# Top-32 attention and a squared-ReLU feed-forward: the next step's pair maxima ahead of the third search round, the far copy between the two exps

## The chip, the cores and the metric

The kernel runs on one core of a Trainium2 chip. The metric is the device time of one execution in microseconds (us), the median of several runs. The core has five engines with instruction queues of their own, each worked off in order: PE (TensorE, matmuls), DVE (VectorE), ACT (ScalarE), POOL (GpSimd) and SP (SyncE, which here issues DMAs). They wait for each other by semaphores.

## What is computed

For 8 batches of 8 heads with 576 rows of 64 values, attention in which each row keeps the 32 largest of its 576 scores; its result, 4608 rows of 512, goes through a feed-forward layer with a squared ReLU.

```python
def _attn_ref(q, k, v):
    top_k = 32
    scale = 1.0 / np.sqrt(D)
    scores = scale * np.matmul(q, k.transpose(0, 1, 3, 2))
    kth = np.partition(scores, -top_k, axis=-1)[..., -top_k:-top_k + 1]
    mask = scores >= kth
    scores = np.where(mask, scores, -1000000000.0)
    scores = scores - np.max(scores, axis=-1, keepdims=True)
    attn = np.exp(scores)
    attn = attn / (np.sum(attn, axis=-1, keepdims=True) + 1e-09)
    return np.matmul(attn, v)

def _moe_ref(x, w_in, w_out):
    h = np.maximum(x @ w_in, 0.0)
    return h * h @ w_out
```

## The kernel before

The 36864 rows of scores are worked in U = 144 steps of 256 rows: two tiles of 128 rows by 576 columns, called x = 0 and 1. `pin` keeps the instructions of each engine in the order in which the program issues them, so the order of the calls in the loop over u is the order of every queue.

**Scores.** In step u the scores of step u + 1 are made (`scores`): PE multiplies the first 288 columns into the PSUM tile sc_a and the other 288 into sc_b, and ACT copies each into the SBUF tile `s` (L299), with its sign turned in most steps (`sign`: positive only for u below 7 and in the last two steps). Between the two halves PE does the products of an older step (`in_gap`). sc_a and sc_b exist once: the next matmul into sc_a waits for its last reader, which is L324 (L322 where the sign is positive), that into sc_b for L353.

**The search for the 32 largest.** A tournament on DVE and POOL writes into the tile `cats`, which has one slot for even and one for odd steps.

- `pairs_of(u+1)` (L324 or L322, DVE): the larger of each column of sc_a and its partner in `s`, 288 for each tile, into `most`. It needs the copy of sc_b into `s`.
- `copy_far(u+1)` (L359, ACT): half of `most` back into the PSUM bank of sc_b.
- `quads_of(u+1)` (L352 and L353, DVE): the larger and the smaller of the two halves of `most`, into `cats`; the first of a step's operations on DVE, and it waits for the far copy.
- `both` (L367) and `lesser` (L375, POOL): sum of the pair less its larger one, which is the smaller one, into `cats`.
- `topk(u, rounds)`: rounds 0, 1 and 2 each find the eight largest (L406) of a part of `cats` for each tile and strike them out there (L410, a match-replace); round 3 finds the last eight. The parts grow: 100, 120, 151 and 368 columns. Before round 2 the eight largest of the lesser ones (L404) are put into columns TOP+QUAR to REST of the slot, which belong to the part of round 2, columns TOP to REST-1.

**After the search.** POOL marks in step u + 1 what falls away (`drop`, L470), and a DMA from POOL's queue adds the mark to `s` (`add_mask`, L474). Some steps later ACT does the exp of the two tiles (`exps`, L482; up to step U - 25 with the sum of each row as a second output, read by an instruction of its own), and SP's queue transposes the result by DMA into `wT` (`turn`, L491). The exps are those of step u - 3, in the last ten of step u - 2. Three, two and in the end again two steps later `products` multiplies wT with the values (`weigh`, L526), DVE takes a reciprocal (`invert`, L542 or L546) and ACT scales (`place`, L565, L570).

**`keep_tops`** (L442, ACT) copies, with its sign turned, the eight largest of round 0 and the eight lesser tops out of `cats` into `m_neg`: in each step where the sign is positive, for both slots at once in every odd step elsewhere. Its reading covers columns 0 to 8 and TOP+QUAR to REST.

**Other work between.** `prepare` puts transposed queries and keys (L180 and others), `dense` two or three pieces of the feed-forward (relu L661 and square L669 on ACT, L654 and L722 on PE) into each step, `fetch` loads the next heads on SP, `run_tests` and the list `tests` are small operations of POOL (L422).

The order of one step in the middle, by engine. DVE: quads, round 0, round 1, L404, round 2, L324 of the next step, round 3; the reciprocal stands ahead of round 1. ACT: copy of sc_a, a transposed x_tok where there is one, copy of sc_b, `prepare`, `place`, exp 0, exp 1, `keep_tops`, far copy, then values and the relu and square pieces. POOL: two drops, `both`, the mask's DMA, a test, `lesser`.

Of the kernel before, what the change touches and what calls it, by code (L numbers as in the profile page):

```python
# [23 lines left out]
def kernel(  # L24
# [9 lines left out]
    nc = tc.nc  # L34
# [8 lines left out]
    HALF, QUAR = S // 2, S // 4  # L43
    EIGHTH = S // 8
    TOP = 8
    REST = TOP + QUAR + 8
    LESS = REST + EIGHTH
    BACK = LESS + QUAR
    WIDE = REST + 3 * QUAR

    def pin(ins):
        tc.keep_in_program_order(ins)
        return ins
# [220 lines left out]
    st = {}  # L274
# [36 lines left out]
    def sign(u):  # L311
        return 1.0 if u < EARLY - 2 or u >= U - 2 else -1.0

    def pairs_of(u):
        d = st[u]
        cat = d["cat"]
        most = d["most"] = scp.tile([128, 2, HALF], f32, name="most", bufs=2)
        one, two = d["ps"][0], d["s"][:, :, HALF:S]

        def tt(to, lo, hi, op):  # L320
            if sign(u) > 0:
                pin(nc.vector.tensor_tensor(to, one[:, :, lo:hi], two[:, :, lo:hi], op=op))  # L322
            else:
                pin(nc.vector.scalar_tensor_tensor(out=to, in0=two[:, :, lo:hi], scalar=-1.0, in1=one[:, :, lo:hi], op0=ALU.mult, op1=op))  # L324

        if u:
            tt(most, 0, HALF, ALU.max)
        else:
            tt(d["ps"][1][:, :, 0:QUAR], QUAR, HALF, ALU.max)
            tt(most[:, :, 0:QUAR], 0, QUAR, ALU.max)  # L330
        if u < EARLY:
            tt(cat[:, :, BACK:BACK + QUAR], QUAR, HALF, ALU.min)
# [23 lines left out]
    def copy_far(u):  # L356
        d = st[u]
        if u:
            pin(nc.scalar.activation(in_two(d["ps"][1][:, :, 0:QUAR]), fours(u)[1], AF.Copy))  # L359
# [20 lines left out]

    def topk(u, rounds=(0, 1, 2, 3)):
        d = st[u]
        g = u % GROUP
        if g == 0 and 0 in rounds:
            held_m["last"] = (held_m.get("m"), held_m.get("neg"))
            held_m["m"] = small.tile([128, GROUP, 2, 3, 8], f32, name="m", bufs=2)
            held_m["neg"] = small.tile([128, GROUP, 2, 2, 8], f32, name="m_neg", bufs=2)
        held = held_m["m"]  # L390
        d["held_neg"] = held_m["neg"]
        m = d["m"] = [d["cat"][:, :, 0:TOP]] + [held[:, g, :, r] for r in range(3)]
        cat = d["cat"]
        def part(r, x):
            if r == 0:
                return cat[:, x, TOP:TOP + QUAR].rearrange("p (g n) -> p g n", n=36)[:, :, 0:25]
            if r == 1:
                return cat[:, x, TOP:TOP + QUAR].rearrange("p (g n) -> p g n", n=36)[:, :, 6:36]
            return cat[:, x, TOP:(REST - 1, BACK)[r - 2]]

        for r in rounds:
            if r == 2:
                for x in range(2):
                    pin(nc.vector.max(out=cat[:, x, TOP + QUAR:REST], in_=cat[:, x, BACK:WIDE]))  # L404
            for x in range(2):
                pin(nc.vector.max(out=m[r][:, x, :], in_=part(r, x)))  # L406
            if r == 3:
                break
            for x in range(2):
                pin(nc.vector.match_replace(out=part(r, x), in_to_replace=m[r][:, x, :], in_values=part(r, x), imm_value=NEG))  # L410
# [3 lines left out]
    def run_tests(u):  # L414
        f0 = 2 * (u + 1 - GROUP)
        both_held = held_m["last"] if u < U - 1 else (held_m["m"], held_m["neg"])
        held, neg = (both_held[z][:, :].rearrange("p g x r j -> p (g x) r j") for z in (0, 1))
        at = flags[:, :, f0:f0 + 2 * GROUP]
        least = held[:, :, 2, 7]

        def test(r, one, two, op):
            tests.append(lambda: pin(nc.gpsimd.tensor_tensor(at[:, r], one, two, op=op)))  # L422

        for r in range(2):
            test(r, least, held[:, :, r, 7], ALU.subtract)
        test(2, least, neg[:, :, 0, 7], ALU.add)
        test(3, held[:, :, 0, 0], neg[:, :, 0, 0], ALU.add)
        test(4, least, neg[:, :, 1, 7], ALU.add)
        test(5, least, least, ALU.mult)
# [46 lines left out]
    def exps(u, x):  # L476
        d = st[u]
        if u % 2 == 0 and x == 0 and u < SUMMED:
            d["sums"] = small.tile([128, 2, 2], f32, name="sums", bufs=4)
            st[u + 1]["sums"] = d["sums"]  # L480
        total = d["sums"][:, u % 2, x:x + 1] if u < SUMMED else None
        pin(nc.scalar.activation(w_two[u % 3][:, x, 0:S], d["s"][:, x, :], AF.Exp, bias=d["less"][x], scale=sign(u), accum_out=total))  # L482
# [55 lines left out]
    def invert(u):  # L538
        if u < SUMMED:
            if u % 2 == 0:  # L540
                both_r = small.tile([128, 2, 2, 1], f32, name="rboth", bufs=4)
                pin(nc.vector.reciprocal(both_r[:, :, :, 0], st[u]["sums"][:, :, :]))  # L542
                st[u]["r"], st[u + 1]["r"] = both_r[:, 0], both_r[:, 1]
            return
        r = small.tile([128, 2, 1], f32, name="rsum", bufs=4)
        pin(nc.vector.reciprocal(r[:, :, :], sums(u)[:, :, 64:65]))  # L546
        st[u]["r"] = r
# [324 lines left out]
    def ok(w):  # L872
        return 0 <= w < U
# [11 lines left out]
    def turn_x(u):  # L885
        for b, c in full:
            x_unit(u, b, c)
        full.clear()

    for u in range(U):  # L890
        at_step[0] = u
        for x in range(2):
            if ok(u - 1) and not by_vector(u - 1, x):
                drop(u - 1, x)
        quads_of(u)
        topk(u, (0,))
        if u == U - 1:
            break
        if ok(u + 1):
            for i, c, a in steps[u + 1]:  # L900
                while coming <= i or (coming == i + 1 and soon):
                    prepare(u)
            scores(u + 1, (lambda: in_gap(u)) if u else None)
            both(u + 1)
            if ok(u - 1) and by_dma(u - 1):
                add_mask(u - 1)
        if u == 0:
            in_gap(u)
        sums_late = ok(to_weigh(u)) and to_weigh(u) >= SUMMED and u < U - 5
        if sums_late:  # L910
            topk(u, (1,))
        if ok(to_weigh(u)):
            invert(to_weigh(u))
        casts_next = bool(soon) and soon[0].__name__ == "values"
        for _ in range(0 if casts_next else 2 if u < 8 else 1):
            prepare(u)
        if ok(to_weigh(u)):
            place(to_weigh(u))
        turn_x(u)
        moves.extend(soon_moves)  # L920
        soon_moves.clear()
        if u < 6:
            fetch(4)
        w = to_raise(u)
        if ok(w):
            exps(w, 0)
            exps(w, 1)
            turn(w)
        if u >= 6:
            fetch(4 if u < 12 else 3)  # L930
        if u and u % GROUP == 0:
            run_tests(u - 1)
        if tests and u % GROUP % 2:
            tests.pop(0)()
        topk(u, (2,) if sums_late else (1, 2))
        if u == U - 2:
            while behind:
                behind.pop(0)()
            take("d")
            products(u - 3)  # L940
            take("d")
        if ok(u + 1):
            pairs_of(u + 1)
            if u == U - 2:
                invert(u - 3)
            if sign(u) > 0:
                keep_tops(u, 1)
            elif u % 2:
                keep_tops(u, 2 if sign(u - 1) < 0 else 1)
            copy_far(u + 1)  # L950
            lesser(u + 1)
        if u == U - 2:
            place(u - 3)
            turn_x(u)
            take("d", True)
            moves.pop(0)()()
        if u == CATCH:
            exps(u - 2, 0)
            exps(u - 2, 1)
            turn(u - 2)  # L960
        topk(u, (3,))
        if casts_next:
            prepare(u)
        while after_far:
            after_far.pop(0)()
        after_far.extend(next_far)
        next_far.clear()
        if u < U - 2:
            dense(u, 0)
        if sign(u) > 0:  # L970
            st[u]["neg"] = negate(u, 3)
        if u in (SOON, CATCH + 1):
            w = to_weigh(u) + 1
            products(w)
            invert(w)
            place(w)
            turn_x(u)
        if u < U - 2:
            dense(u, 1)
        else:  # L980
            early_exps(u, 1)
        load_weights(1 if u else 2)
# [15 lines left out]
    exps(U - 2, 0)  # L998
    early_exps(U - 1, 0)
    early_exps(U - 1, 1)  # L1000
    topk(U - 1, (1, 2, 3))
    one.bits(8)
    mask(U - 2, 1)
    mask(U - 1, 0)
# [194 lines left out]
```

## Time and profile before

| | |
|---|---|
| median of 3 runs | 860.99 us (860.27 to 893.82) |
| the profiled execution's own time | 865.61 us |
| its span, first to last instruction | 863.8 us |
| mean granted TensorE clock in it | 0.959 |
| busy: DVE, ACT, POOL, PE | 819.9, 780.4, 770.6, 662.4 us |
| steps | 144 |

The profile is of one execution. Busy time is that of the instructions themselves; an engine's idle time is put down to what released it, which is inferred from semaphores. A line number is that of the listing above; where two shapes share a line, the shape tells them apart. In a timeline each row is one instruction, or several alike that follow each other (x2); the number in brackets at its end is the idle time just before it. DVE's instructions overlap a little with the one before, so start to start is shorter than the duration.

### The profile page before, as it was taken

To read this page: it belongs to the slowest core of one execution; us is meant where nothing else is said; L and a number is where in the kernel's file an instruction comes from. 1 tells how busy PE (TensorE), PEld (TensorE's weight loads), DVE (VectorE), ACT (ScalarE), POOL (GpSimd) and SP (SyncE) were. 2 spreads that over 40 slices of the span, in tenths; PEclk is the share of its full clock that TensorE was granted. 3 is DMA by queue.
4 is the path that set the end of the run, shared out by engine and by line. 5 is a ranking of instruction groups with operands and counts; after the bars stand their busy time and mean duration, and the time that the engine had idled before them with its cause. 6 is when DMAs were issued, how large, how long until landed. Compare 5 with 4: busy or idle time off the path is not lost.

```text
span 863.8 us, 20769 instructions
## 1 busy us (share of the span) xinstructions
PE 662.4 (77%) x6213; PEld 419.8 (49%) x6282; DVE 819.9 (95%) x3717; ACT 780.4 (90%) x1945; POOL 770.6 (89%) x830
## 2 busy tenths in 40 slices
PE   6787777877777877777787777777777878888886
PEld 3334344554555545444454454554444555555554
DVE  5999999998899999999999999999999999999994
ACT  4677799997999999999999999999999999999893
POOL 7999989997899999999899999999989998888881
PEclk9989999997999999999999999999999999999999
DMA  9999998799988999999988999989999998688861
GB/s 178 156 144 198 181 202 201 175 184 166 251 209 187 215 212 210 213 188 204 226 206 205 205 209 214 206 195 212 218 190 215 217 211 211 162 159 181 171 155 43
DMA packets 291064, 165.96 MB, mean 192 GB/s; under 512 B 258176, under 2 KB 268672, under 8 KB 290944
## 3 DMA queue, kind: packets, MB, share of 16 engines
q1 hardware_dynamic: 267408, 80.29, 51.3%
q0 software_dynamic: 22192, 83.83, 41.1%
q8 instruction: 52, 0.85, 0.4%
q14 instruction: 68, 0.56, 0.2%
q10 hardware_dynamic: 1344, 0.43, 0.2%
HBM read 37.75 MB, written 9.44 MB: 55 GB/s over the span
## 4 chain that ended last, share of the span: by engine, by line
DVE 41%; ACT 19%; issue 7%; PE 4%; DMA 4%; POOL 1%; ACTq 0%; DVEq 0%; POOLq 0%
DVE m L406 13%; DVE cats L410 12%; DVE cats L404 5%; DVE cats L352 3%; DVE cats L353 3%; ACT s L299 3%; DVE cats L406 3%; ACT w_two_c L482 2%; DMA wT<-w_two_b 2%; ACT w_two_a L482 2%; ACT rl L661 2%; ACT x_tok L565 2%; ACT w_two_b L482 2%; DMA wT<-w_two_c 2%; ACT sc_b L359 1%
## 5 line engine op out<-in xcount | busy, mean ns | idle before, releaser
L406 DVE MAX8 m<-cats 128x8 f32<-128x120 f32 (+2 forms) x864 | 281.6, 369 | 0.0
L367 POOL TENSOR_TENSOR cats<-s 128x576 int32<-128x576 int32 (+1 forms) x144 | 197.4, 1371 | 44.4 <-ACT s L299 37.0
L375 POOL TENSOR_TENSOR cats<-cats,most 128x576 int32<-128x576 int32 (+1 forms) x144 | 235.0, 1632 | 1.1 <-DVE most L324 0.2
L654 PEld LDWEIGHTS <-w_in 128*128 128x128 bf16 x2304 | 146.2, 101 | 41.2 <-issue 17.6
L290 PE MATMUL sc_a<-qkT 64*128 64x288 f32 x512 | 98.4, 462 | 86.5 <-DVE most L324 82.4
L410 DVE MATCH_REPLACE8 cats<-m,cats 128x120 f32<-128x120 f32 (+1 forms) x576 | 159.8, 286 | 0.0
L290 PE MATMUL sc_b<-qkT 64*128 64x288 f32 x512 | 103.9, 480 | 60.4 <-DVE cats L353 55.6
L722 PE MATMUL dn_ps<-w_out,h 128*128 128x512 bf16 x478 | 134.4, 400 | 9.7 <-issue 4.9
L654 PE MATMUL gen<-xT,w_in 128*128 128x128 bf16 x1984 | 136.5, 225 | 6.9 <-ACT xT L609 3.6
L299 ACT ACTIVATE s<-sc_b 128x576 f32<-128x576 f32 x144 | 93.4, 648 | 30.0 <-PE sc_b L290 25.4
L324 DVE SCALAR_TENSOR_TENSOR most<-s,sc_a 128x576 f32<-128x576 f32 x135 | 100.9, 747 | 0.7 <-ACT s L299 0.6
L299 ACT ACTIVATE s<-sc_a 128x576 f32<-128x576 f32 x144 | 91.4, 634 | 9.0 <-PE sc_a L290 7.2
L404 DVE MAX8 cats<-cats 128x8 f32<-128x216 f32 x288 | 95.3, 374 | 1.6 <-POOL cats L375 1.6
L290 PEld LDWEIGHTS sc_a<-qkT 64*128 64x128 f32 x512 | 39.9, 189 | 116.6 <-DVE most L324 99.8
L669 ACT ACTIVATE h<-rl 128x512 bf16<-128x512 f32 x136 | 85.7, 630 | 4.3
L661 ACT ACTIVATE rl<-gen 128x512 f32<-128x512 f32 x140 | 83.0, 593 | 2.4 <-PE gen L654 2.0
L526 PEld LDWEIGHTS <-wT 128*128 128x128 bf16 (+1 forms) x1600 | 55.1, 100 | 59.0 <-issue 46.8
L352 DVE TENSOR_TENSOR cats<-sc_b,most 128x288 f32<-128x288 f32 x144 | 64.6, 448 | 17.4 <-ACT sc_b L359 16.0
L290 PEld LDWEIGHTS sc_b<-qkT 64*128 64x128 f32 x512 | 43.3, 195 | 75.4 <-PE av_ps L526 40.9
L722 PEld LDWEIGHTS <-h 128*128 128x128 bf16 x544 | 49.9, 102 | 60.1 <-issue 24.6
L482 ACT ACTIVATE w_two_b<-s,m_neg 128x576 bf16<-128x576 f32 x95 | 72.5, 783 | 4.2 <-DMA s<-gone_b 2.3
L470 POOL TENSOR_SCALAR gone_a<-s,m 128x576 uint8<-128x576 f32 x90 | 66.9, 743 | 8.5
(203 smaller groups left out, 1487.2 us busy)
## 6 DMA issues: line engine op xcount, KB each, us to landing
s<-gone_b POOLq DMA_DIRECT2D x45, 576.0 KB, 4.8
s<-gone_c POOLq DMA_DIRECT2D x45, 576.0 KB, 4.8
s<-gone_a POOLq DMA_DIRECT2D x45, 576.0 KB, 4.4
v_raw<-in_v_dram SPq DMA_DIRECT2D x64, 128.0 KB, 3.3
k_raw<-in_k_dram SPq DMA_DIRECT2D x63, 128.0 KB, 3.9
q_raw<-in_q_dram SPq DMA_DIRECT2D x63, 128.0 KB, 4.2
out_dram<-wide SPq DMA_DIRECT2D x31, 256.0 KB, 3.4
v_raw<-in_v_dram SPq DMA_DIRECT2D x64, 32.0 KB, 3.9
```

Source lines behind the costliest of these rows:

```text
L290: pin(nc.tensor.matmul(out=ps[j][:, x, 0:HALF], lhsT=lhsT, rhs=rhs, start=True, stop=True))
L299: pin(nc.scalar.activation(s[:, :, j * HALF:(j + 1) * HALF], ps[j][:, :, 0:HALF], AF.Copy, scale=sign(u)))
L324: pin(nc.vector.scalar_tensor_tensor(out=to, in0=two[:, :, lo:hi], scalar=-1.0, in1=one[:, :, lo:hi], op0=ALU.mult, op1=op))
L367: pin(tt(less, s[:, :, 0:wide].bitcast(i32), s[:, :, HALF:HALF + wide].bitcast(i32), op=ALU.add))
L375: pin(tt(less, less, d["most"][:, :, 0:wide].bitcast(i32), op=ALU.subtract))
L404: pin(nc.vector.max(out=cat[:, x, TOP + QUAR:REST], in_=cat[:, x, BACK:WIDE]))
L406: pin(nc.vector.max(out=m[r][:, x, :], in_=part(r, x)))
L410: pin(nc.vector.match_replace(out=part(r, x), in_to_replace=m[r][:, x, :], in_values=part(r, x), imm_value=NEG))
L482: pin(nc.scalar.activation(w_two[u % 3][:, x, 0:S], d["s"][:, x, :], AF.Exp, bias=d["less"][x], scale=sign(u), accum_out=total))
L654: pin(nc.tensor.matmul(out=hp[:, n * n_rows:(n + 1) * n_rows], lhsT=w_in[:, kh, (f0 + n) * 128:(f0 + n + 1) * 128], rhs=xt(kh), start=(kh ...
L661: pin(nc.scalar.activation(kept["rl"][:, :], hp, AF.Relu))
L722: pin(nc.tensor.matmul(out=op[:, :], lhsT=held["h2"][:, f, c * 128:(c + 1) * 128], rhs=w_out[:, f, :], start=(f == 0), stop=(f == NF - 1)))
```

## The change

Three calls change places within a step of the loop; what each computes is as before.

- The eight lesser tops (L404) become a function of their own, `lesser_tops(u)`, which is called between rounds 1 and 2, where they were.
- `next_pairs(u)` holds what stood after round 2: `pairs_of(u+1)`, `keep_tops`, `copy_far(u+1)` and `lesser(u+1)`. It is now called right after `lesser_tops(u)`, ahead of round 2.
- The second exp and the transposing DMA (`exps(w, 1)`, `turn(w)`) and the loads of `fetch` come after `next_pairs(u)`. So on ACT `keep_tops` and the far copy stand between the two exps, and on DVE L324 stands ahead of round 2.
- In step U - 2 `next_pairs` keeps its old place, and the search of step U - 1 has its old order.

```diff
--- before.py
+++ after.py
@@ -380,6 +380,11 @@
 
 
 
+    def lesser_tops(u):
+        cat = st[u]["cat"]
+        for x in range(2):
+            pin(nc.vector.max(out=cat[:, x, TOP + QUAR:REST], in_=cat[:, x, BACK:WIDE]))
+
     def topk(u, rounds=(0, 1, 2, 3)):
         d = st[u]
         g = u % GROUP
@@ -399,9 +404,6 @@
             return cat[:, x, TOP:(REST - 1, BACK)[r - 2]]
 
         for r in rounds:
-            if r == 2:
-                for x in range(2):
-                    pin(nc.vector.max(out=cat[:, x, TOP + QUAR:REST], in_=cat[:, x, BACK:WIDE]))
             for x in range(2):
                 pin(nc.vector.max(out=m[r][:, x, :], in_=part(r, x)))
             if r == 3:
@@ -886,6 +888,17 @@
         for b, c in full:
             x_unit(u, b, c)
         full.clear()
+
+    def next_pairs(u, between=None):
+        pairs_of(u + 1)
+        if between:
+            between()
+        if sign(u) > 0:
+            keep_tops(u, 1)
+        elif u % 2:
+            keep_tops(u, 2 if sign(u - 1) < 0 else 1)
+        copy_far(u + 1)
+        lesser(u + 1)
 
     for u in range(U):
         at_step[0] = u
@@ -924,32 +937,28 @@
         w = to_raise(u)
         if ok(w):
             exps(w, 0)
+        if u and u % GROUP == 0:
+            run_tests(u - 1)
+        if tests and u % GROUP % 2:
+            tests.pop(0)()
+        if not sums_late:
+            topk(u, (1,))
+        lesser_tops(u)
+        if u < U - 2:
+            next_pairs(u)
+        if ok(w):
             exps(w, 1)
             turn(w)
         if u >= 6:
             fetch(4 if u < 12 else 3)
-        if u and u % GROUP == 0:
-            run_tests(u - 1)
-        if tests and u % GROUP % 2:
-            tests.pop(0)()
-        topk(u, (2,) if sums_late else (1, 2))
+        topk(u, (2,))
         if u == U - 2:
             while behind:
                 behind.pop(0)()
             take("d")
             products(u - 3)
             take("d")
-        if ok(u + 1):
-            pairs_of(u + 1)
-            if u == U - 2:
-                invert(u - 3)
-            if sign(u) > 0:
-                keep_tops(u, 1)
-            elif u % 2:
-                keep_tops(u, 2 if sign(u - 1) < 0 else 1)
-            copy_far(u + 1)
-            lesser(u + 1)
-        if u == U - 2:
+            next_pairs(u, lambda: invert(u - 3))
             place(u - 3)
             turn_x(u)
             take("d", True)
@@ -998,7 +1007,9 @@
     exps(U - 2, 0)
     early_exps(U - 1, 0)
     early_exps(U - 1, 1)
-    topk(U - 1, (1, 2, 3))
+    topk(U - 1, (1,))
+    lesser_tops(U - 1)
+    topk(U - 1, (2, 3))
     one.bits(8)
     mask(U - 2, 1)
     mask(U - 1, 0)
```

## Rows read from the trace of the kernel before

**Rows 1.** The page, busy us of each engine, share of the span, instructions.
```profile
PE 662.4 (77%) x6213; PEld 419.8 (49%) x6282; DVE 819.9 (95%) x3717; ACT 780.4 (90%) x1945; POOL 770.6 (89%) x830
```

**Rows 2.** Waits of DVE: engine, line, releaser, us in total, times, longest.
```profile
DVE cats L352 <- ACT sc_b L359: 16.0, 24, 2.1
```

**Rows 3.** Waits of ACT, the same columns.
```profile
ACT s L299 <- PE sc_a L290: 7.2, 13, 1.7
...
ACT m_neg L442 <- DVE cats L410: 1.5, 2, 1.0
```

**Rows 4.** Groups by line and form: count, busy us, mean ns, idle before.
```profile
L367 POOL TENSOR_TENSOR cats<-s 128x576 int32<-128x576 int32 x135 | 190.2, 1409 | 41.0 <-ACT s L299 33.7
```

**Rows 5.** Timeline of DVE around three steps: start us, duration us, instruction, idle before.
```profile
399.31 0.45 DVE L353 TENSOR_TENSOR cats<-sc_b,most 128x288 f32<-128x288 f32 x1
...
401.91 0.52 DVE L406 MAX8 m<-cats 128x8 f32<-128x151 f32 x2
402.35 0.07 DVE L410 MATCH_VALUE_LOAD cats<-m,cats 128x8 f32 x1
...
402.91 0.75 DVE L324 SCALAR_TENSOR_TENSOR most<-s,sc_a 128x576 f32<-128x576 f32 x1
403.57 0.98 DVE L406 MAX8 m<-cats 128x8 f32<-128x368 f32 x2
404.52 0.46 DVE L352 TENSOR_TENSOR cats<-sc_b,most 128x288 f32<-128x288 f32 x1
...
410.12 0.45 DVE L352 TENSOR_TENSOR cats<-sc_b,most 128x288 f32<-128x288 f32 x1
...
414.73 0.99 DVE L406 MAX8 m<-cats 128x8 f32<-128x368 f32 x2
415.63 0.45 DVE L352 TENSOR_TENSOR cats<-sc_b,most 128x288 f32<-128x288 f32 x1
```

**Rows 6.** Timeline of ACT in the first of those steps.
```profile
401.00 0.64 ACT L299 ACTIVATE s<-sc_b 128x576 f32<-128x576 f32 x1
401.53 0.60 ACT L180 ACTIVATE qkT<-gen 128x512 f32<-128x512 f32 x1
...
403.16 0.79 ACT L482 ACTIVATE w_two_b<-s,m_neg 128x576 bf16<-128x576 f32 x1
...
403.91 0.27 ACT L442 ACTIVATE m_neg<-cats 128x64 f32<-128x64 f32 x1
404.06 0.43 ACT L359 ACTIVATE sc_b<-most 128x288 f32<-128x288 f32 x1
```

**Rows 7.** Timelines of DVE and ACT in one of the last steps.
```profile
762.79 0.45 DVE L353 TENSOR_TENSOR cats<-sc_b,most 128x288 f32<-128x288 f32 x1
...
765.82 0.65 ACT L299 ACTIVATE s<-sc_b 128x576 f32<-128x576 f32 x1
...
766.51 0.75 DVE L324 SCALAR_TENSOR_TENSOR most<-s,sc_a 128x576 f32<-128x576 f32 x1
...
768.08 0.28 ACT L442 ACTIVATE m_neg<-cats 128x64 f32<-128x64 f32 x1
...
768.69 0.46 DVE L352 TENSOR_TENSOR cats<-sc_b,most 128x288 f32<-128x288 f32 x1 [0.53 <-ACT sc_b L359]
```

**Rows 8.** Timelines of DVE and POOL where L324 and L367 run together.
```profile
749.22 0.76 DVE L324 SCALAR_TENSOR_TENSOR most<-s,sc_a 128x576 f32<-128x576 f32 x1
...
749.26 1.41 POOL L367 TENSOR_TENSOR cats<-s 128x576 int32<-128x576 int32 x1 [1.30 <-ACT s L299]
```

**Rows 9.** Timelines of SP's queue and PE: a late transpose and its first user.
```profile
768.23 2.93 SPq L491 DMA_TRANSPOSE wT<-w_two_c  x1
...
776.85 0.48 PE L526 MATMUL av_ps<-vau_c,wT 128*128 128x65 bf16 x10 [1.05 <-DMA wT<-w_two_c]
```

**Rows 10.** Timeline of DVE: the first and last L352 of the 142 steps.
```profile
16.85 0.44 DVE L352 TENSOR_TENSOR cats<-sc_b,most 128x288 f32<-128x288 f32 x1
...
836.18 0.44 DVE L352 TENSOR_TENSOR cats<-sc_b,most 128x288 f32<-128x288 f32 x1
```

## The prediction

> **What bounds the kernel now.** I read the busy shares first. VectorE (DVE) works for 819.9 of 863.8 us, ScalarE (ACT) for 780.4, GpSimd (POOL) for 770.6 [rows 1]: three engines close together, DVE ahead. So a gain can only come out of DVE's idle time, and a loss comes as soon as DVE waits for an engine that has little to spare itself.
>
> DVE's list of waits comes next. One wait stands out: `quads_of` (L352) for the far copy of ACT (L359), 16.0 us in 24 waits [rows 2]. Third, the timeline of single steps. A step runs from one L352 to the next. An undisturbed one takes 5.51 us (410.12 to 415.63) [rows 5]; from the first L352 shown (16.85) to the last (836.18) 142 steps take 819.3 us, or 5.77 each [rows 10]. At 5.55 a step, with 0.36 more in the first seven for a second operation of `pairs_of`, 142 steps would need some 791 us. The rest, 29 us, is DVE waiting, some 27 of it for the two copies of ACT that are followed below. That is more than the 16.0 of the list, because a wait shorter than the running maximum's tail is swallowed by its busy time: in the step from 398.93 the two last maxima take 0.95 (403.57 to 404.52) where an undisturbed pair takes 0.90 (414.73 to 415.63) [rows 5].
>
> Fourth, ACT in the same step [rows 6]. It copies the scores of sc_b into `s` (L299, ending 401.64), then the copy of `prepare` (L180), then `place`, the first and the second exp (L482, the second at 403.16), `keep_tops` (L442, 403.91) and the far copy (L359, 404.06, ending 404.49). L352 starts at 404.52, 0.03 later: here the chain that sets the step is ACT's, from the copy of sc_b.
>
> **The change, part by part.** Nothing is added or removed; four groups change places.
>
> *The pair maxima (L324) go ahead of the third round.* DVE's sum stays: each DVE instruction starts where the one before lets it, and none of the new neighbours reads what its direct forerunner writes. L324 starts 1.00 earlier relative to the rounds (401.91 to 402.91 is the third round) [rows 5]. It needs the copy of sc_b, so that copy's deadline comes 1.00 earlier. In the shown step L324 could start at 401.91, and the copy ended at 401.64: no wait, 0.27 to spare. In the late step it ended at 766.47, 3.23 after the end of L353 (763.24), and L324 ran at 766.51 [rows 7]. L324's new place is 401.91 − 399.76 = 2.15 after L353's end, so a step like the late one waits up to 1.08 there that before it did not.
>
> *The lesser tops (L404) stay* between the second and the third round: L404's position to POOL's `lesser` is as before. Cost nothing. POOL's order (drops, `both`, the mask's DMA, a test, `lesser`) is also as before.
>
> *L324 beside POOL.* It now runs while POOL does `both` (L367). I take zero: with L324 at 749.22 and L367 at 749.26, L367 took 1.41 [rows 8], and its mean over 135 is 1409 ns [rows 4]. The bound on the other side would be L324's 0.66 on L367 in each of 134 steps, 88 us, and this row excludes it. The Trainium skill, "SBUF — State Buffer", section "SBUF: two separate sides", says that a DVE operation with two SBUF inputs and a GpSimd operation lock each other out for a whole instruction; read for any operation with two tensors, that would speak against this move. L324 takes one of its two from PSUM (sc_a), and by the rule as by the row it is free.
>
> *sc_a is freed 1.00 earlier.* ACT waited for PE's sc_a scores for 7.2 us in all [rows 3]; that is the most this can give, and nothing is the least. I take nothing, because most of ACT's copies of sc_a stand behind ACT's own relu and square.
>
> *Far copy ahead of the second exp.* The second exp's 0.75 (403.16 to 403.91) [rows 6] leaves the chain from sc_b's copy to L352 and comes behind the far copy. That is what can save the 16.0 us. It does not make ACT shorter: where ACT is behind, the exp is paid before the next step's copy of sc_b.
>
> *The transposing DMA (`turn`, SP's queue)* follows the second exp and comes later by the far copy, 0.43 at most [rows 6]. Behind it on SP stand the loads of `fetch` and the stores of `wide`; neither is needed within the step. Its product is: in the late steps the matmuls of `weigh` follow two steps after, and at 776.85 one waited 1.05 for a transpose issued at 768.23 [rows 9]. Bounds: nothing, or 0.43 in each of the last 21 steps (9 us). I take 0.4 us, for one such step.
>
> *A wait that the change makes.* `keep_tops` (L442) reads the lesser tops in columns TOP+QUAR to REST of `cats`; the third round's match-replace (L410) overwrites TOP to REST−1. They overlap. Before, `keep_tops` was issued after that L410 and waited for it: ACT's list has exactly this pair, L442 for L410 [rows 3]. After, it is issued ahead of it, so the order turns round: **DVE's L410 of the third round must wait until ACT's L442 has read.** This holds in each odd step, and in each of the first seven. Behind the waiting L410 stand the last maxima, L352, and through them POOL's drops and PE's next sc_b.
>
> Price in the shown step: L324 starts 401.91, the next instruction 0.66 later (402.91 to 403.57), L410's value load 0.44 after that (401.91 to 402.35): 403.01 [rows 5]. L442 starts at 403.91 − 0.75 = 403.16, ends 0.27 later at 403.43 [rows 6]; with 0.04 for the signal 403.47. **DVE waits 0.46.** From there 0.56 (402.35 to 402.91) and 0.90 to L352: 404.93 instead of 404.52. The far copy is long done (403.16 + 0.15 + 0.43), so its wait is gone and a longer one stands in its place: +0.41 for this step.
>
> In general this wait is (end of the sc_b copy + p + 0.04) − (start of L324 + 1.10), where p is ACT's way from that copy to L442's end without the second exp: 1.79 here, 1.22 in the late step (768.08 − 766.47 − 0.67 + 0.28, the late exps being 0.67 without their accumulator) [rows 6, 7]. With a prepared copy in the way (p about 1.8) it is 0.1 to 0.3 where sc_b comes early and 0.7 where it is just in time or late; without one it is nothing to 0.2.
>
> **The sum.** The same working, from step to step, each carrying ACT's place into the next, over the 142 steps from 16.85 to 836.18 [rows 10]:
> Waits before: 24.7 at L352 (16.0 of them in the list) and 2.1 at L324, together 26.8.
> After, at L410: 15.6 in the 35 odd middle steps with a prepared copy, 2.5 in the 22 without, 1.6 in the first seven, 2.1 in the last 21: 21.9.
> After, at L324: 5.0 in odd and 1.6 in even middle steps, 8.0 in the last 21, 0.2 early: 14.8. At L352 1.6 are left.
> 38.4 − 26.8 = **+11.6 us**. With 0.05 more or less for the signal the sum runs from +7 to +14.
>
> The profiled execution took 865.61 us (span 863.8), 4.6 above the median of 860.99. A stretch around 200 us in which PE ran slow holds 6 of its waits and 0.9 of the 11.6. Without it, and with the 0.4 for the transposes, the median goes from 861.0 to **872 us**, 1.3% slower.
>
> **Rivals.**
> *The wait is hidden* (0.20). If L442 ends within 1.10 of L324's start, the L410 term is nothing. For it: without a prepared copy it is nearly so. Against it: the shown step misses it by 0.42 before any signal [rows 5, 6]. What is left is 14.8 + 1.6 against 26.8, but without L410's wait DVE runs ahead of ACT and meets sc_b late in more steps and for longer: the same working without the L410 term gives −2 us, 859.
> *The far copy's waits simply go* (0.08). L352's 16.0 vanish and nothing takes their place: 845 us; with the hidden ones 836. For it: the largest wait on the list. Against it: the deadline of sc_b, 1.00 earlier, already missed in the late step [rows 7]. It decides if the copy of sc_b comes within 2.15 of L353 in nearly all steps.
> *The transposes come late too* (0.15). The 0.43 in each of the last 21 steps, and the next copies of sc_b late behind PE, add 9 to the 11: 881 us. For it the 1.05 of [rows 9], against it that few products waited at all.
> My forecast has 0.57.
>
> **How the numbers follow.** The range takes in the hidden wait below and the late transposes above, 857 to 881; what is left out is the case of 845 and the upper half of the last one. The forecast's own range is 867 to 876. Two per cent, about what a measurement of this kernel tells from no change, is 17 us: faster than 844 is the better half of the second rival, 0.03; slower than 878 is the third with a share of the forecast's tail, 0.17; in between 0.80.
>
> **What would show it.** DVE's list: L352 for L359 falls from 16.0 to under 3; a new line, L410 for ACT's L442, of about 22 us in some 60 waits, all in odd steps or the first seven; L324 for ACT's L299 appears with some 15, half of it in the last 21 steps. DVE's busy sum stays at 820, L367 at 1.41. The forecast is wrong if L410 shows no wait for L442, or if the odd and the even steps are equally long.

## The result: 872.4 us, 1.3% slower, odd steps longer and even ones shorter

The changed kernel takes 872.36 us (median of 6 runs, 870.40 to 876.23) where the kernel before, beside it, takes 861.73: a ratio of 1.013, 95% interval 1.011 to 1.015. In a later series it was 872.57 against 862.26, 1.013 (1.009 to 1.016). By two per cent that is no change; the intervals leave no doubt that it is slower. A run more than 1.5% above the fastest of the same kernel counts in the medians and not in the ratios. The granted TensorE clock is not what differs: the profiled execution of the later series had 0.960, that of before 0.959.

The profiled execution of the changed kernel took 873.15 us, its span is 871.3. Lines below 386 have kept their numbers. The lesser tops are now L386, the rounds' maxima L408, their match-replaces L412 (L410 before), `keep_tops` L444 (L442), the exps L484 (L482).

The page of the changed kernel, busy us, share of the span, instructions; [rows 1] is its like:

```profile
PE 667.2 (77%) x6213; PEld 424.8 (49%) x6282; DVE 822.2 (94%) x3717; ACT 781.5 (90%) x1945; POOL 770.5 (88%) x830
```

DVE, ACT and POOL do the same work within 2.3 us; the time that was added is waiting. DVE's list of waits for L324 in the kernel before (us in total, times, longest):

```profile
DVE most L324 <- ACT s L299: 0.6, 2, 0.3
```

and DVE's list in the changed kernel:

```profile
DVE cats L412 <- ACT m_neg L444: 11.5, 26, 0.7
DVE most L324 <- ACT s L299: 9.2, 18, 1.6
...
DVE most L322 <- ACT s L299: 1.6, 2, 1.2
```

The line of [rows 2], L352 for the far copy with its 16.0 us, is gone from the list. Two others stand in its place: the match-replace that waits for `keep_tops`, and L324, which waits for the copy of sc_b (0.6 us before).

The timeline of DVE in the step from 400.96, the same step of the computation as the first of [rows 5]:

```profile
400.96 0.43 DVE L352 TENSOR_TENSOR cats<-sc_b,most 128x288 f32<-128x288 f32 x1
...
403.93 0.73 DVE L324 SCALAR_TENSOR_TENSOR most<-s,sc_a 128x576 f32<-128x576 f32 x1
404.58 0.52 DVE L408 MAX8 m<-cats 128x8 f32<-128x151 f32 x2
405.51 0.09 DVE L412 MATCH_VALUE_LOAD cats<-m,cats 128x8 f32 x1 [0.41 <-ACT m_neg L444]
405.59 0.30 DVE L412 MATCH_REPLACE8 cats<-m,cats 128x151 f32<-128x151 f32 x1
...
406.10 0.98 DVE L408 MAX8 m<-cats 128x8 f32<-128x368 f32 x2
406.99 0.44 DVE L352 TENSOR_TENSOR cats<-sc_b,most 128x288 f32<-128x288 f32 x1
...
412.57 0.44 DVE L352 TENSOR_TENSOR cats<-sc_b,most 128x288 f32<-128x288 f32 x1
```

and of ACT in it, beside [rows 6]:

```profile
403.04 0.64 ACT L299 ACTIVATE s<-sc_b 128x576 f32<-128x576 f32 x1
403.57 0.60 ACT L180 ACTIVATE qkT<-gen 128x512 f32<-128x512 f32 x1
...
404.44 0.80 ACT L484 ACTIVATE w_two_b<-s,m_neg 128x576 bf16<-128x576 f32 x1
405.11 0.23 ACT L484 ACTIVATION_READ_ACCUMULATOR w_two_b<-s,m_neg 128x1 f32 x1
405.20 0.28 ACT L444 ACTIVATE m_neg<-cats 128x64 f32<-128x64 f32 x1
405.35 0.44 ACT L359 ACTIVATE sc_b<-most 128x288 f32<-128x288 f32 x1
```

L444 ends at 405.48; DVE's value load begins at 405.51, 0.03 later. The step is 6.03 us long (400.96 to 406.99), the even one after it 5.58 (406.99 to 412.57). The far copy ended at 405.79, 1.2 us ahead of the L352 that needs it: it comes early, as the change wanted, but it is no longer what DVE waits for.

Read from one L352 to the next, for all steps: the 57 odd steps of the middle (9 to 121) took 325.6 us before and 339.8 after, +14.2; the 57 even ones 325.2 and 318.1, −7.0; the last 21 126.8 and 126.2; the first seven 41.7 and 41.9. 1.2 us were lost before the first step of these. Five of the middle steps (31 to 35) lay in a slow stretch of the profiled execution of before, 33.8 against 30.3 us; there the granted TensorE clock was 0.70 of full speed from 200 to 210 us and 0.66 from 210 to 220. Without them the odd steps grew by 14.5 us and the even ones shrank by 3.8. The two profiled executions lie 7.5 us apart (865.61 and 873.15), without these five steps 11.1, near the distance of the medians (10.6).

### The profile page after: what moved, and what is told of

Read it like the earlier page. It is cut to its first block, busy times and chain, and to the rows that moved or that the text cites. A ratio compares the mean times of both kernels' runs of the same rounds, so it can differ in the third digit from the quotient of the medians.

```text
span 871.3 us, 20844 instructions
## 1 busy us (share of the span) xinstructions
PE 667.2 (77%) x6213; PEld 424.8 (49%) x6282; DVE 822.2 (94%) x3717; ACT 781.5 (90%) x1945; POOL 770.5 (88%) x830
## 4 chain that ended last, share of the span: by engine, by line
DVE 38%; ACT 31%; PE 15%; issue 10%; DMA 4%; POOL 1%; SPq 1%; ACTq 0%; DVEq 0%
DVE cats L412 11%; DVE m L408 10%; ACT s L299 6%; PE sc_b L290 6%; DVE cats L353 4%; DVE cats L352 4%; ACT x_tok L567 4%; ACT w_two_c L484 3%; DVE most L324 3%; ACT w_two_b L484 3%; ACT w_two_a L484 3%; DVE cats L386 3%; ACT rl L663 3%; PE gen L656 2%; PE sc_a L290 2%
## 5 line engine op out<-in xcount | busy, mean ns | idle before, releaser
L408 DVE MAX8 m<-cats 128x8 f32<-128x120 f32 (+2 forms) x864 | 281.8, 368 | 0.0
L367 POOL TENSOR_TENSOR cats<-s 128x576 int32<-128x576 int32 (+1 forms) x144 | 197.6, 1372 | 52.1 <-ACT s L299 47.5
L375 POOL TENSOR_TENSOR cats<-cats,most 128x576 int32<-128x576 int32 (+1 forms) x144 | 238.2, 1654 | 0.7
L656 PEld LDWEIGHTS <-w_in 128*128 128x128 bf16 x2304 | 150.9, 103 | 42.0 <-issue 20.5
L412 DVE MATCH_REPLACE8 cats<-m,cats 128x120 f32<-128x120 f32 (+1 forms) x576 | 159.1, 284 | 0.1
L724 PE MATMUL dn_ps<-w_out,h 128*128 128x512 bf16 x478 | 138.9, 410 | 10.1 <-issue 5.1
L656 PE MATMUL gen<-xT,w_in 128*128 128x128 bf16 x1984 | 139.6, 228 | 5.5 <-ACT xT L611 2.8
L299 ACT ACTIVATE s<-sc_b 128x576 f32<-128x576 f32 x144 | 93.5, 649 | 41.6 <-PE sc_b L290 32.2
L290 PE MATMUL sc_a<-qkT 64*128 64x288 f32 x512 | 100.5, 471 | 11.4 <-DVE most L324 10.2
L324 DVE SCALAR_TENSOR_TENSOR most<-s,sc_a 128x576 f32<-128x576 f32 x135 | 99.7, 739 | 9.3 <-ACT s L299 9.2
L386 DVE MAX8 cats<-cats 128x8 f32<-128x216 f32 x288 | 94.9, 371 | 1.6 <-POOL cats L375 1.6
L484 ACT ACTIVATE w_two_a<-s,m_neg 128x576 bf16<-128x576 f32 x96 | 75.2, 784 | 0.7 <-DMA s<-gone_a 0.7
L484 ACT ACTIVATE w_two_b<-s,m_neg 128x576 bf16<-128x576 f32 x95 | 74.0, 779 | 1.2 <-issue 1.2
L472 POOL TENSOR_SCALAR gone_c<-s,m 128x576 uint8<-128x576 f32 x90 | 66.9, 743 | 8.5
```

The costliest lines, as they stand in the source:

```text
L290: pin(nc.tensor.matmul(out=ps[j][:, x, 0:HALF], lhsT=lhsT, rhs=rhs, start=True, stop=True))
L299: pin(nc.scalar.activation(s[:, :, j * HALF:(j + 1) * HALF], ps[j][:, :, 0:HALF], AF.Copy, scale=sign(u)))
L367: pin(tt(less, s[:, :, 0:wide].bitcast(i32), s[:, :, HALF:HALF + wide].bitcast(i32), op=ALU.add))
L375: pin(tt(less, less, d["most"][:, :, 0:wide].bitcast(i32), op=ALU.subtract))
L472: pin(nc.gpsimd.tensor_scalar(byte[:, x, :], s[:, x, :], scalar1=d["m"][3][:, x, 7:8], scalar2=HUGE, op0=ALU.add, op1=ALU.mult))
L656: pin(nc.tensor.matmul(out=hp[:, n * n_rows:(n + 1) * n_rows], lhsT=w_in[:, kh, (f0 + n) * 128:(f0 + n + 1) * 128], rhs=xt(kh), start=(kh ...
```

## The experiments

Two rivals stand against the wait of the match-replace: that the earlier deadline of sc_b's copy costs the time (L324's 9.2 us), and that the second exp and the transpose behind it come too late. On the chip of the first four runs (the two with `keep_tops` elsewhere, the pair maxima with both exps ahead of `keep_tops`, and the far copy alone) most runs of the kernel before lay between 862 and 874 us, so their medians are read against 862.3 (before) and 872.6 (changed) of the second group, and the ratios measured beside them are given too.

### keep_tops behind the third round again

The lines that call `keep_tops` go from `next_pairs` into a function `keep(u)`, and this is called behind the third round:

```diff
     def next_pairs(u, between=None):
...
-        if sign(u) > 0:
-            keep_tops(u, 1)
-        elif u % 2:
-            keep_tops(u, 2 if sign(u - 1) < 0 else 1)
...
         topk(u, (2,))
+        keep(u)
```

> The changed order, but keep_tops (ACT) is issued behind the third round's match-replace again, as in the kernel before. Theory (the new wait of L410 for keep_tops costs the time): the changed kernel's waits of L410 for ACT's keep_tops (11.5 us in 26) are gone, L324's waits for the copy of sc_b grow a little (9.2 to about 13 us), and the time falls from 872 to about 858, 3 below the kernel before (range 855 to 862). Rival 1 (the earlier deadline of the sc_b copy costs it): L410's wait was only the same lateness seen later in the step, L324's wait takes it over, time stays at 868 to 873. Rival 2 (the second exp and the transpose come too late): nothing changes for them, 870 to 874.

Measured: 858.51 us (858.15 to 861.66; 0.989 of the kernel before, 0.983 to 0.995). Its DVE waits, the same columns:

```profile
DVE most L324 <- ACT s L299: 11.1, 22, 1.6
```

The wait for `keep_tops` is gone and 14 us with it. L324's wait grew by 1.9 us and did not take its place. Both rivals fall as the cause of the loss: sc_b's deadline is here as in the changed kernel, and so is the place of the second exp (0.15 us earlier, since `keep_tops` now stands behind it).

### keep_tops ahead of the first exp

`next_pairs` is without `keep_tops` here too.

```diff
+        if not sums_late:
+            topk(u, (1,))
+        lesser_tops(u)
+        if u < U - 2:
+            keep(u)
         w = to_raise(u)
         if ok(w):
             exps(w, 0)
...
-        if not sums_late:
-            topk(u, (1,))
-        lesser_tops(u)
```

> The changed order, but keep_tops stands ahead of the first exp on ACT, so that it reads the lesser tops 0.75 us sooner and the match-replace behind it need not wait. The far copy and the second exp stay where the change put them. Theory: L410's wait falls from 11.5 to 0 to 3 us, L324's wait is 10 to 14 us, time 859 (856 to 863). Rival 1 (sc_b's deadline): 868 to 873. Rival 2 (late transposes): 870 to 874.

Measured: 859.34 us (857.45 to 860.70; 0.988, 0.980 to 0.996). Its DVE waits:

```profile
DVE most L324 <- ACT s L299: 12.8, 24, 1.6
...
DVE cats L412 <- ACT m_neg L444: 0.3, 1, 0.3
```

Here the match-replace does stand behind `keep_tops`, as in the changed kernel, but that one comes 0.75 us sooner, and the wait falls from 11.5 us in 26 to 0.3 in one. It is the lateness of the read that costs, not the order as such.

### The pair maxima alone, both exps ahead of keep_tops

```diff
         if ok(w):
             exps(w, 0)
+            exps(w, 1)
+            turn(w)
...
         if u < U - 2:
             next_pairs(u)
-        if ok(w):
-            exps(w, 1)
-            turn(w)
```

> Only the first half of the change: L324 and next_pairs ahead of the third round, but both exps ahead of keep_tops and the far copy on ACT, as before. Theory: the match-replace of the third round now waits for a keep_tops that stands behind both exps, 0.75 us later in each odd step; L410's waits grow from 11.5 us to 40 to 65 us, in nearly all 71 odd steps, and the time is 895 to 918. Rival 1 (only sc_b's deadline): L324's waits as in the changed kernel, 864 to 873. Rival 2 (late transposes): the exps are back, so 860 to 863.

Measured: 922.15 us (920.06 and 924.25; 1.061, 1.050 to 1.072). DVE's waits, and then DVE's and ACT's timelines in one odd step:

```profile
DVE cats L412 <- ACT m_neg L444: 62.8, 71, 1.9
...
DVE most L324 <- ACT s L299: 4.9, 10, 1.0
DVE cats L352 <- ACT sc_b L359: 4.0, 9, 0.6
```

```profile
404.07 0.78 ACT L484 ACTIVATE w_two_a<-s,m_neg 128x576 bf16<-128x576 f32 x1
404.74 0.21 ACT L484 ACTIVATION_READ_ACCUMULATOR w_two_a<-s,m_neg 128x1 f32 x1
404.83 0.26 ACT L444 ACTIVATE m_neg<-cats 128x64 f32<-128x64 f32 x1
...
405.12 0.09 DVE L412 MATCH_VALUE_LOAD cats<-m,cats 128x8 f32 x1 [0.88 <-ACT m_neg L444]
```

With `keep_tops` one exp later the wait grows to 62.8 us, and the time by 50 us over the changed kernel (4 over the upper end of what was expected). It takes place 71 times, and the middle steps show where: 6.64 us an odd step, 5.67 an even one. The granted clock was lower here, 0.921, but DVE did not wait more for PE's scores: L324 waits 4.9 us for the copy of sc_b, where it is 9.2 in the changed kernel. That the rounds' order alone were the cause would have left this kernel at 864 to 873.

### The pair maxima alone, with nothing waiting for keep_tops

Again `next_pairs` is without `keep_tops`.

```diff
             exps(w, 0)
+            exps(w, 1)
+            turn(w)
...
         topk(u, (2,))
+        keep(u)
```

> L324 ahead of the third round as in the changed kernel, both exps ahead of the far copy as before the change, and keep_tops behind the third round, so that no match-replace waits for it. Against the run with the first half of the change alone only keep_tops is moved. Theory: the 62.8 us that L410 waited there are gone, L324 waits some 6 to 10 us, L352 still about 9 us for the far copy, time 861 (858 to 865), as the kernel before: what the pair maxima's move takes at L324 it gives back at L352. Rival (the earlier deadline of sc_b alone makes the kernel slower): 866 to 873.

Measured: 864.34 us, the median of ten runs from 859.39 to 879.39 (the profiled one took 861.65); 1.002 of the kernel before (0.998 to 1.006). DVE's waits:

```profile
DVE most L324 <- ACT s L299: 8.5, 17, 1.5
...
DVE cats L352 <- ACT sc_b L359: 3.6, 11, 0.6
```

Between the last two kernels only the place of `keep_tops` differs: 58 us. The move of the pair maxima by itself is worth nothing that these runs can tell: 8.5 us at L324 stand against what L352 no longer waits (16.0 before, 3.6 here, where about 9 was expected).

### The far copy alone

```diff
         lesser_tops(u)
+        topk(u, (2,))
         if u < U - 2:
             next_pairs(u)
         if ok(w):
             exps(w, 1)
             turn(w)
...
-        topk(u, (2,))
```

> Only the second half of the change: the far copy and keep_tops stand between the two exps on ACT, but L324 stands behind the third round as before. Theory: keep_tops reads after the third round again, so there is no wait of L410, and the copy of sc_b has its old deadline; L352's 16.0 us of waits fall to about 8, ACT waits a little for L324. Time 856 (853 to 860). Rival 1 (sc_b's deadline is what cost the time): the same, 853 to 860. Rival 2 (the late transposes cost it): as slow as the changed kernel, 868 to 874.

Measured: 856.31 us (854.12 to 857.65; 0.986, 0.980 to 0.992). DVE's waits, then ACT's longest:

```profile
DVE most L324 <- ACT s L299: 4.0, 7, 1.0
DVE cats L352 <- ACT sc_b L359: 3.5, 10, 0.6
```

```profile
ACT sc_b L359 <- DVE most L324: 17.5, 42, 0.9
```

This half of the change is a gain by itself: L352's wait falls from 16.0 to 3.5 us (8 was expected). ACT now often reaches the far copy before L324 is done and waits, 17.5 us in all; DVE's 3.5 at L352 is much less, so most of that waiting did not hold DVE up. The second exp and the transpose come late here too, in a kernel faster than the one before: it is shown twice that they are not what costs.

### The changed kernel again, and two places between

> The changed kernel as it is, for a comparison with the next three on one chip. Both theories expect what was measured: about 872 us (868 to 878), L410 waiting about 11 us for keep_tops in the list of waits.

Measured: 872.57 us, 1.013 (1.009 to 1.016). DVE's waits:

```profile
DVE cats L412 <- ACT m_neg L444: 12.0, 25, 1.1
DVE most L324 <- ACT s L299: 8.4, 18, 1.6
```

The next kernel calls `next_pairs`, without `keep_tops`, from within the third round, between its maxima and its match-replaces, and `keep` behind it; the second exp stays behind the far copy.

```diff
-        if u < U - 2:
-            next_pairs(u)
+        topk(u, (2,), (lambda: next_pairs(u)) if u < U - 2 else None)
         if ok(w):
             exps(w, 1)
             turn(w)
...
-        topk(u, (2,))
+        keep(u)
...
             for x in range(2):
+                if between and x == 0:
+                    between()
                 pin(nc.vector.match_replace(...))
```

> L324 between the maxima and the match-replaces of the third round (0.57 us instead of 1.00 earlier than before the change), the far copy between the exps, keep_tops behind the third round. Theory: no wait of L410; L324 waits for sc_b about 9 us instead of 11, L352 about 3; time 855 (852 to 858), the fastest or level with the version that moves the far copy alone (856.3). Rival (any earlier L324 costs, so the far copy alone is best): 857 to 860.

Measured: 854.72 us (854.31 to 857.47), 0.992 (0.989 to 0.995). With `x == 1` instead, between the two match-replaces:

> As the run before this one, with L324 between the two match-replaces of the third round (0.29 us earlier than before the change). Theory: L324 waits about 7 us, L352 about 5, time 854 (851 to 858). Rival (any earlier L324 costs): 856.5 to 859.

Measured: 856.17 us, 0.992 (0.989 to 0.995). That is within the theory's range and 0.3 us below the rival's, and decides nothing by itself. And the far copy alone and the first of these two once more, on one chip:

> The far copy alone moved, once more, beside the next run on one chip, since the two had been measured on different ones. Theory (an L324 some 0.6 us earlier trades about 5 us of waits at L352 for about 5 at L324): the two are level, 854 to 857.5 both, within 1.5 us of each other. Rival (any earlier L324 costs): this one is faster by 2 us or more.

> L324 between the maxima and the match-replaces of the third round, the far copy between the exps, keep_tops behind the third round, once more. Theory: level with the run before, 854 to 857.5. Rival: slower than that by 2 us or more.

Measured: 856.42 us for the far copy alone (0.992, 0.989 to 0.996) and 854.54 with L324 in the middle of the third round (0.991, 0.988 to 0.994), DVE's waits in the latter:

```profile
DVE most L324 <- ACT s L299: 7.1, 13, 1.6
...
DVE cats L352 <- ACT sc_b L359: 0.6, 1, 0.6
```

That an L324 earlier by 0.57 us costs 2 us or more, as the rival had it, is refuted; whether it gains against the far copy alone is not settled: the medians lie 1.9 us apart, a little more than the 1.5 that was expected for level, while the runs of the two overlap. The far copy alone and these two places are faster than the kernel before, by some 6 to 9 us, and than the changed one, by some 16 to 18.

## Why the prediction was right, step by step

*The new wait.* Predicted from an overlap of columns and from ACT's order: DVE's match-replace waits for `keep_tops`, in odd steps and the first seven. The list names this pair, and the runs with `keep_tops` elsewhere take it away or multiply it. In the step worked out in advance the wait was to be 0.46, from start to start, and the step 6.00 us long (404.93 − 398.93). The wait was 0.48 (405.51 less 403.93 and the 1.10 of the prediction), of which 0.41 shows as idle time, and the step 6.03.

*The sum.* +11.6 against the profiled execution of before, +11 between the medians; the medians moved by 10.6, the profiled executions by 7.5, chiefly because the working carried the slow stretch over into the changed kernel, where it did not come again. The terms can be counted as in the prediction, from the start of one instruction to the start of the next, less what the same two take undisturbed. After the change that gives 18.6 us at the match-replace (21.9 predicted), 11.5 at L324 and L322 (14.8) and nothing at L352 (1.6); before it, 21.3 at L352 (24.7) and 1.1 at L324 (2.1). So every term was somewhat too large. Outside steps 31 to 35 both sides of the sum come out some 4 us below the working, 16.3 for 20.8 before and 27.6 for 31.5 after, and the difference, 11.3 for 10.7, survived: that the total agrees so well owes something to like errors on both sides.

*What was mis-sized.* I wrote that DVE's list would show about 22 us in some 60 waits at the match-replace, and 15 at L324. It shows 11.5 in 26, and 10.8 with L322's. The interval count finds 18.6 in 57 waits at the match-replace. Of the 7.1 between, 4.7 are swallowed by the tail of the instruction in front, 0.08 each time, which is the very thing the prediction says of L352's 16.0 for 24.7; I did not apply it to the lines that I foretold. The other 2.4 are idle times of 0.12 us or less in 31 waits, which the list leaves out. L324's waits were to lie half in the last 21 steps, 8.0 us; there they were 4.9, and in the odd middle steps 6.4 instead of 5.0. Another 1.2 went in the very first step, where L322 waits for the copy of sc_b and which the working did not cover.

*Costed at nothing.* L324 beside POOL's L367 [rows 4, 8]: in the changed kernel the group is

```profile
L367 POOL TENSOR_TENSOR cats<-s 128x576 int32<-128x576 int32 x135 | 190.4, 1411 | 48.6 <-ACT s L299 44.1
```

1411 ns against 1409. The prediction takes it for new that the two run together. It is not: they did in 130 of the 135 steps before, for 64 us in all; now it is 130 steps and 94 us, and L367 takes no longer for it (403.93 and 403.77 in the step shown, L367's row there being 1.41 as well). The earlier release of sc_a gave nothing that can be seen, as taken: ACT's wait for sc_a fell from 7.2 to 3.9 us, and its wait for sc_b grew from 25.4 to 32.2. The late transposes: the 0.4 us taken for them is too small to be seen in any run; the range to 9 us is excluded by the far copy alone at 856.

*The rivals.* "The wait is hidden" priced a kernel without that wait at −2 us, 859; with `keep_tops` moved away it was 858.5 and 859.3. So that price was right, and only its condition did not hold. "The far copy's waits simply go" gave 836 to 845; no run came near. In the first experiment L352's wait is indeed gone and L324's is 11.1: the deadline of sc_b takes back most of the gain, as the prediction had it.

## What to carry to other kernels

When an instruction is moved ahead of a reader of the same columns on another engine, look for the pair in the list of waits of before: the same two lines, with reader and writer exchanged, are the wait to come, and its price is how late the reader stands in its own queue. A small reading (0.28 us in the step shown) between two long instructions of a nearly full engine can cost more than the move gains: 14 us here, where the same order without that wait gained about 4. Where two halves of a change share a call, measure each alone: here one was a gain of 0.8%, the other nothing, and what rode along with them, `keep_tops`, made the loss. Look, too, at what the reader needs: by the listing, of the eight lesser tops that `keep_tops` copies into `m_neg` a later instruction reads only the eighth (`neg[:, :, 1, 7]` in `run_tests`), and the third round's part, `cat[:, x, TOP:REST - 1]`, ends one column short of it. Whether a `keep_tops` that copies that one alone would be free of the wait is not shown; no run tried it.

## What the runs showed that I had not expected

PE's two largest waits changed places, and their sum hardly moved (152.8 us before, 158.1 after). Before, in PE's list:

```profile
PE sc_a L290 <- DVE most L324: 94.7, 105, 2.3
PE sc_b L290 <- DVE cats L353: 58.1, 110, 2.0
```

and in the changed kernel:

```profile
PE sc_b L290 <- DVE cats L353: 147.4, 114, 2.1
PE sc_a L290 <- DVE most L324: 10.7, 39, 1.3
```

The earlier L324 took 84 us from PE's wait before sc_a, and PE then stood 89 us longer before sc_b, which L353 releases. And in this kernel the match-replace waits already with the load of its eight values, 0.08 us (405.51 to 405.59) ahead of the write that must not come early: the wait is that of the whole pair.
